# Moving the first six scalings of a float64-to-float32 weight conversion from ScalarE to GpSimd

## The chip, the cores and the metric

The kernel runs on one core of one Trainium2 chip. The metric is the device time of one execution in microseconds (us). Three runs of the kernel before gave 615.62, 618.41 and 619.05 us; the median is 618.41 us. The engines are named as the profile names them: PE (TensorE), PEld (its weight loads), DVE (VectorE), ACT (ScalarE), POOL (GpSimd) and SP (SyncE, which issues most DMAs). A trailing q (SPq) is an engine's queue.

## The reference, cut to what matters

Three layers follow each other: attention with capped scores (4 batches, 12 heads, 448 tokens, 64 per head), a feed-forward layer with a squared ReLU (768 to 2048 to 768), and a soft mixture of 8 experts.

```python
scores = scale * np.matmul(q, k.transpose(0, 1, 3, 2))
scores = cap * np.tanh(scores / cap)
attn = softmax(scores)                 # written out in the reference
x = attn @ v                           # to (1792, 768)
h = x @ w_in                           # w_in, w_out: float64
r = np.maximum(h, 0.0)
x = (s * (r * r) + b) @ w_out
...                                    # soft mixture: phi, w1, w2
```

`w_in` and `w_out` arrive as float64. The kernel turns them into float32 itself, with integer operations on the two 32-bit words of each number.

## The kernel before, in words

**Attention.** Heads are taken in twelve groups of four, Q = 0 to 11, three for each batch. A group makes score tiles `sc` on PE (lines 148, 170, 178), their tanh on ACT (lines 158, 160, 182), the exponentials on ACT (line 220), their sum `es` on DVE (lines 229 and 233), the products with v in `U` on PE (line 261), the column sums `Sm` on PE, copied with a small constant added on ACT (line 246), a reciprocal on DVE (line 247) and a product that gives the group's part of x (lines 275 to 279). Queries and keys are first split into a high and a low half on DVE, later partly on ACT (lines 94 and 95). Queues run in order on every engine.

**Feed-forward.** For each batch, `hidden` runs 16 chunks of the 2048 columns. A chunk splits its slice of `w_in` (tile `wr`) into `ws`, high half on ACT (line 540), low half on DVE (line 541), and makes 18 products into `hp` on PE (line 557). The first of them needs the x of batch 0, that is groups Q = 0, 1, 2. The attention of the next batch is interleaved with the chunks of this one. Then come the last batch without attention, and a tail that reads the weights of the experts (tile `wt`, 48 transfers of 1 MB).

**Conversion.** `convert` (line 375 on) is a generator that is advanced between those steps. A unit is a tile `raw` of 128 x 768 float64 numbers, loaded by SP (line 391) into one of three buffers. ACT takes the high words as float32, scales them by 2 to the -112 and writes `wr` or `o` (line 397, `scale`). DVE masks and shifts the result (line 402, `first`), puts the sign back (line 426) and adds the low word's bits (line 430), which frees the raw buffer. There are 48 units: 16 slices of `w_in` (stored for the later batches at line 461), 16 halves of `w_out` transposed and 16 of `w_out`. The first six in the order of the program are `w_in` slices 0 and 1, the two halves of the first transposed `w_out` part (tile `o`), and `w_in` slices 2 and 3. Unit 4 in the program's count, the fifth, has a condition: it is issued after the instruction `self.mark`, the exponential of group Q = 2, chunk 3 (set in `expo`). The order of instructions on the engines is a scheduler's, from the dependencies and the priorities in the code.

Of the kernel before, what the change touches and what calls it, by code (L numbers as in the profile page):

```python
# [7 lines left out]
F32 = mybir.dt.float32  # L8
# [3 lines left out]
AF = mybir.ActivationFunctionType  # L12
ALU = mybir.AluOpType
# [34 lines left out]
CU = 768  # L48
LAY = (22, 3, 2)
HOLD = 4  # L50
FAR = 2
ORDER = (0, 2, 4, 1, 3, 5)
XPOS = (1, 4, 7, 10, 13, 15, 15, 15)
# [10 lines left out]
class Body:  # L64
# [184 lines left out]
    def weighted(self, Q, chunks):  # L249
# [6 lines left out]
        for k in order:  # L256
            for h in range(2):
                for i in range(4):
                    d = (i % 2 * KF + k if k < KF else 2 * KF) * D + 32 * h
                    j = 32 * (i ^ 2 * h if Q >= FAR * NQ else i)  # L260
                    products.append(lambda k=k, h=h, i=i, j=j, d=d: nc.tensor.matmul(  # L261
# [4 lines left out]
    def finish(self, Q):  # L266
# [6 lines left out]
        with self.tc.high_priority(100) if Q < NQ else nullcontext():  # L273
            if Q < FAR * NQ:
                nc.vector.tensor_mul(out, u, self.rec[:, None, :].to_broadcast([P, 2, S]))
# [103 lines left out]
    def convert(self, units):  # L379

        nc = self.nc
        N = len(units)
        raw, out = {}, {}

        def load(n):
            if n < N:
                raw[n] = self.cv.tile([P, CU, 2], I32, tag="raw", bufs=self.raws, name="raw")  # L390
                nc.sync.dma_start(raw[n].rearrange("p a b -> p (a b)"), units[n][0].bitcast(I32))

        def scale(n):
            if n < N:
                out[n] = units[n][1]()
                with self.tc.issue_after(self.mark) if n == 4 and self.mark else nullcontext():
                    nc.scalar.activation(out[n], raw[n][:, :, 1].bitcast(F32), AF.Copy, scale=2.0 ** -112)  # L397

        def first(n):
            if n < N:  # L400
                o = out[n].bitcast(I32)
                nc.vector.tensor_scalar(o, o, 0x0FFFFFFF, 3, op0=ALU.bitwise_and, op1=ALU.logical_shift_left)

        for n in range(self.raws - 1):
            load(n)
        for n in range(N + 1):
            if n:
                units[n - 1][2](out.pop(n - 1))
            late = n < N and n not in out
            for _ in range(HOLD if self.later and late else 0):  # L410
                yield
            while self.later and (late or n == N):
                self.later.pop(0)()
                yield
            if late:
                while not units[n][3]():
                    yield
                scale(n)
                first(n)
            load(n + self.raws - 1)  # L420
            ahead = n + 1 < N and units[n + 1][3]()
            if ahead:
                scale(n + 1)
            if n < N:
                o = out[n].bitcast(I32)
                nc.vector.scalar_tensor_tensor(o, raw[n][:, :, 1], -0x80000000, o, op0=ALU.bitwise_and, op1=ALU.bitwise_or)  # L426
            if ahead:
                first(n + 1)
            if n < N:
                nc.vector.scalar_tensor_tensor(o, raw.pop(n)[:, :, 0], 29, o, op0=ALU.logical_shift_right, op1=ALU.bitwise_or)  # L430
            yield
            while self.later:
                self.later.pop(0)()
                yield
# [77 lines left out]
    def w_need(self, i):  # L512
# [6 lines left out]
        else:  # L519
            self.wr[i] = self.raw_slice()  # L520
            src, n = self.wsc[i % FC] if self.f64 else self.io["w_in"][i % FC], KC * P // 2
            if i < FAR * FC:
                self.nc.sync.dma_start(self.wr[i], src)
# [581 lines left out]
```

## Time and profile before

| what | value |
|---|---|
| median of three runs | 618.41 us (615.62 to 619.05) |
| the profiled execution's own time | 618.13 us |
| its span, first to last instruction | 616.3 us |
| PE, DVE, ACT, POOL busy | 573.2, 382.7, 394.2, 4.1 us |
| mean granted TensorE clock | 0.984 |
| chain that ended last, by engine | PE 47%, DMA 17%, DVE 16%, ACT 13%, issue 5% |

The span is 1.8 us shorter than the execution's own time; what lies around it is the same start and end for both kernels. The shares of busy time are averages over stages that have different limits, so the table is only a beginning: which engine has no free time is read stage by stage. "Idle before" in a row is the time in which the engine stood still ahead of that instruction, with what ended it behind the arrow.

### The profile page before, as it was taken

Reading aid. Unit: us, or ns where it says so; the run is one execution under the profiler, and the core shown is the slowest. Engines: PE = TensorE matmul, PEld = TensorE weight load, DVE = VectorE, ACT = ScalarE, POOL = GpSimd, SP = SyncE. Lnnn points to the kernel's source line nnn. Section 1 sums busy time; section 2 is a strip of 40 time slices with the busy share of each in tenths; the row PEclk is TensorE's granted clock in tenths of the full one; section 3 lists DMA queues with packets and bytes.
Section 4 is the critical chain, followed back from the end, with each engine's and each line's share of the span. In section 5 each row is a group of like instructions: output and inputs, shape, how many; then the busy total and the mean of one; then the engine's idle time right before and its main releaser. Section 6 shows DMA issues by size and latency. Waiting matters only on the chain.

```text
span 616.3 us, 11164 instructions
## 1 busy us (share of the span) xinstructions
PE 573.2 (93%) x4488; PEld 386.5 (63%) x4488; DVE 382.7 (62%) x569; ACT 394.2 (64%) x611; POOL 4.1 (1%) x11
## 2 busy tenths in 40 slices
PE   7898999999999999989999999999999998999663
PEld 5243575657677576566875675858788874348543
DVE  4999999999894978748829867462422224213212
ACT  5899889889769688488697696946455541012001
POOL 1000000000000000000000000000000000000000
PEclk9999999999999999989999999999999999999977
DMA  8844768686684665556655632214979989999997
GB/s 293 282 136 144 265 237 294 223 296 220 203 293 155 223 214 160 171 199 194 202 186 173 208 118 75 69 53 151 349 256 307 342 316 365 417 420 414 420 412 279
DMA packets 49995, 149.97 MB, mean 243 GB/s; under 512 B 5504, under 2 KB 27792, under 8 KB 43024
## 3 DMA queue, kind: packets, MB, share of 16 engines
q1 hardware_dynamic: 49648, 148.66, 68.5%
q8 instruction: 37, 0.61, 0.4%
q0 software_dynamic: 288, 0.53, 0.2%
q14 instruction: 22, 0.18, 0.1%
HBM read 131.07 MB, written 18.09 MB: 242 GB/s over the span
## 4 chain that ended last, share of the span: by engine, by line
PE 47%; DMA 17%; DVE 16%; ACT 13%; issue 5%; SPq 1%; DVEq 0%; ACTq 0%
PE hp L557 24%; DMA wt<-in_w_dram 12%; PE U L261 6%; ACT e L220 4%; PE pt L682 2%; PE tp L587 2%; ACT e L182 2%; DVE ws L541 2%; ACT e L158 2%; PE sc L148 2%; DVE o L426 2%; PE sc L178 2%; DVE es L229 2%; PE L L601 1%; DVE rec L247 1%
## 5 line engine op out<-in xcount | busy, mean ns | idle before, releaser
L557 PE MATMUL hp<-x,ws 128*128 128x448 f32 x1152 | 269.2, 377 | 0.0
L557 PEld LDWEIGHTS hp<-x,ws 128*128 128x128 f32 x1152 | 208.1, 189 | 45.7 <-issue 30.6
L541 DVE TENSOR_TENSOR ws<-wr,ws 128x384 fp32r<-128x384 f32 x128 | 70.4, 553 | 88.1 <-ACT ws L540 81.1
L540 ACT CAST ws<-wr 128x384 fp32r<-128x384 f32 x128 | 65.6, 518 | 39.0 <-PE hp L557 38.3
L261 PE MATMUL U<-e,v 128*32 128x448 f32 (+1 forms) x672 | 69.0, 542 | 4.7 <-ACT e L220 3.6
L220 ACT ACTIVATE e<-e,c_acap 128x1792 f32<-128x1792 f32 (+1 forms) x42 | 71.2, 1696 | 0.5
L261 PEld LDWEIGHTS U<-e,v 128*32 128x32 f32 (+1 forms) x672 | 20.5, 109 | 42.9 <-issue 32.7
L590 ACT COPY g<-tp 128x384 f32<-128x384 f32 (+1 forms) x64 | 34.4, 538 | 13.2 <-PE tp L587 7.4
L565 ACT ACTIVATE r<-hp 128x448 f32<-128x448 f32 x63 | 34.4, 545 | 11.0 <-PE hp L557 9.9
L158 ACT ACTIVATE e<-sc,c_tsc 128x896 f32<-128x896 f32 x36 | 35.5, 1005 | 8.9 <-PE sc L148 8.9
L182 ACT ACTIVATE e<-sc,c_tsc 128x896 f32<-128x896 f32 x36 | 35.8, 1024 | 5.7 <-PE sc L178 5.5
L247 DVE RECIPROCAL rec<-rec 128x448 f32<-128x448 f32 x12 | 35.4, 2948 | 5.0 <-ACT rec L246 4.9
L566 ACT ACTIVATE r<-r 128x448 f32<-128x448 f32 x63 | 37.1, 588 | 0.5
L397 ACT ACTIVATE o<-raw 128x768 f32<-128x768 f32 x32 | 29.1, 931 | 12.2 <-DVE c_hh L693 7.4
L958 PE MATMUL so_ps<-wt,free 128*32 128x128 f32 x768 | 27.7, 295 | 9.2 <-DMA wt<-in_w_dram 9.2
L587 PE MATMUL tp<-c_cst,r 128*128 128x128 f32 x192 | 32.6, 277 | 3.6 <-ACT g L590 2.8
L942 ACT COPY wt<-op 128x512 f32<-128x512 f32 (+1 forms) x12 | 6.8, 568 | 42.6 <-PE op L937 42.5
L229 DVE TENSOR_TENSOR es<-e 128x1792 f32<-128x1792 f32 x12 | 24.3, 2022 | 14.1 <-ACT e L220 14.1
L587 PEld LDWEIGHTS tp<-c_cst,r 128*128 128x128 f32 x192 | 23.9, 141 | 12.7 <-ACT g L590 4.7
L430 DVE SCALAR_TENSOR_TENSOR o<-raw,o 128x768 int32<-128x768 int32 x32 | 30.4, 952 | 0.4
L426 DVE SCALAR_TENSOR_TENSOR o<-raw,o 128x768 int32<-128x768 int32 x32 | 30.4, 953 | 0.3
L958 PEld LDWEIGHTS so_ps<-wt,free 128*32 128x32 f32 x768 | 21.8, 117 | 13.3 <-DMA wt<-in_w_dram 9.5
(187 smaller groups left out, 695.0 us busy)
## 6 DMA issues: line engine op xcount, KB each, us to landing
wt<-in_w_dram SPq DMA_DIRECT2D x48, 1024.0 KB, 14.6
raw<-in_w_in_dram SPq DMA_DIRECT2D x16, 768.0 KB, 5.7
raw<-in_w_outT_dram SPq DMA_DIRECT2D x16, 768.0 KB, 5.8
raw<-in_w_out_dram SPq DMA_DIRECT2D x16, 768.0 KB, 5.7
wsc<-wr SPq DMA_DIRECT2D x16, 384.0 KB, 2.8
wr<-wsc SPq DMA_DIRECT2D x16, 384.0 KB, 3.4
osc<-o SPq DMA_DIRECT2D x16, 384.0 KB, 3.5
wr<-wsc SPq DMA_DIRECT2D x32, 192.0 KB, 3.2
```

Source lines behind the costliest of these rows:

```text
L158: nc.scalar.activation(self.e[Q][c][:, 2 * j:2 * j + 2, :], sc[:, :, :S], AF.Tanh, scale=self.c["tsc"])
L182: nc.scalar.activation(self.e[Q][c][:, 2 * j:2 * j + 2, :], sc[j][:, :, :S], AF.Tanh, scale=self.c["tsc"])
L220: ins = self.nc.scalar.activation(e, e, AF.Exp, scale=self.c["acap"]).ins
L247: nc.vector.reciprocal(self.rec, self.rec)
L261: products.append(lambda k=k, h=h, i=i, j=j, d=d: nc.tensor.matmul(self.U[j:j + 32, h, :S], self.v[2 * Q + i // 2][self.rows(i, k), d:d + ...
L426: nc.vector.scalar_tensor_tensor(o, raw[n][:, :, 1], -0x80000000, o, op0=ALU.bitwise_and, op1=ALU.bitwise_or)
L540: self.nc.scalar.copy(hi, u)
L541: self.nc.vector.tensor_sub(lo, u, hi.bitcast(F32))
L557: nc.tensor.matmul(hp[:, :S], ws[kc // 3][:, w, kc % 3, :], x[ORDER[kc] // 2][:, s, ORDER[kc] % 2, :], start=(k == 0), stop=(k == 3 * KC - 1))
L566: self.mark = nc.scalar.activation(r2, r2, AF.Square).ins
L587: nc.tensor.transpose(tp[:, q * P:(q + 1) * P], r2[:, 64 * odd + q * P:64 * odd + (q + 1) * P], self.c["idn"])
L958: nc.tensor.matmul(so_ps[32 * e:32 * e + 32, G, :], ht[G][:, f, 32 * e:32 * e + 32], w2[f // 4][:, f % 4, e, :], start=(f == 0), stop=(f = ...
```

## The change

In the conversion's `scale`, the first six units (n = 0 to 5) are scaled by a GpSimd `tensor_scalar` multiplication by the same constant; the other 42 stay on ACT. The condition on the fifth unit is gone. Nothing else is edited.

```diff
+SIDE = 6
...
         def scale(n):
             if n < N:
                 out[n] = units[n][1]()
-                with self.tc.issue_after(self.mark) if n == 4 and self.mark else nullcontext():
-                    nc.scalar.activation(out[n], raw[n][:, :, 1].bitcast(F32), AF.Copy, scale=2.0 ** -112)
+                if n < SIDE:
+                    nc.gpsimd.tensor_scalar(out[n], raw[n][:, :, 1].bitcast(F32), 2.0 ** -112, None, op0=ALU.mult)
+                    return
+                nc.scalar.activation(out[n], raw[n][:, :, 1].bitcast(F32), AF.Copy, scale=2.0 ** -112)
```

The scheduler moves other instructions too. In the listings below the changed file's lines are numbered 1 to 3 higher than before's (line 220 is 221, line 402 is 405, line 430 is 433), and the numbers behind names tell buffers apart.

POOL, from its last start-up DMA on, before:

```order
L1024 DMA c_misc_100<-in_phi_dram 128x192
L1035 TENSOR_LOAD c_flag_90
L1036 COMPARE_AND_BRANCH
L853 DMA c_misc_100<-in_cst_dram 128x256
L875 DMA free_5080<-in_cst_dram 128x256
```

and now:

```order
L1027 DMA c_misc_100<-in_phi_dram 128x192
L1038 TENSOR_LOAD c_flag_90
L1039 COMPARE_AND_BRANCH
L398 ISA
L398 TENSOR_SCALAR wr_243<-raw_239 128x768
L398 TENSOR_SCALAR wr_248<-raw_241 128x768
L398 TENSOR_SCALAR o_309<-raw_246 128x768
L398 TENSOR_SCALAR o_309<-raw_307 128x768
L398 TENSOR_SCALAR wr_708<-raw_361 128x768
L398 TENSOR_SCALAR wr_715<-raw_706 128x768
```

[...]

ACT in the first group of heads, from the exponential of chunk 0 to that of chunk 2, before:

```order
L220 ACTIVATE e_209<-e_209,c_acap_87 128x1792
L158 ACTIVATE e_235<-sc_228,c_tsc_92 128x896
L158 ACTIVATE e_235<-sc_253,c_tsc_92 128x896
L397 ACTIVATE wr_243<-raw_239 128x768
L220 ACTIVATE e_235<-e_235,c_acap_87 128x1792
L397 ACTIVATE wr_248<-raw_241 128x768
L158 ACTIVATE e_286<-sc_279,c_tsc_92 128x896
L158 ACTIVATE e_286<-sc_289,c_tsc_92 128x896
L397 ACTIVATE o_309<-raw_246 128x768
L220 ACTIVATE e_286<-e_286,c_acap_87 128x1792
```

and now:

```order
L221 ACTIVATE e_209<-e_209,c_acap_87 128x1792
L159 ACTIVATE e_235<-sc_228,c_tsc_92 128x896
L159 ACTIVATE e_235<-sc_253,c_tsc_92 128x896
L221 ACTIVATE e_235<-e_235,c_acap_87 128x1792
L159 ACTIVATE e_286<-sc_279,c_tsc_92 128x896
L159 ACTIVATE e_286<-sc_289,c_tsc_92 128x896
L221 ACTIVATE e_286<-e_286,c_acap_87 128x1792
```

Three scalings are gone from between the attention's own instructions here, a fourth a few rows later, and the two that stood behind the marked exponential as well.

DVE in the same place, from the first unit's mask to the second sum, before:

```order
L402 TENSOR_SCALAR wr_243<-wr_243 128x768
L426 SCALAR_TENSOR_TENSOR wr_243<-raw_239,wr_243 128x768
L430 SCALAR_TENSOR_TENSOR wr_243<-raw_239,wr_243 128x768
L229 TENSOR_TENSOR es_201<-e_209,e_235 128x1792
L402 TENSOR_SCALAR wr_248<-wr_248 128x768
L94 CAST qh_327<-q2_215 128x448
L426 SCALAR_TENSOR_TENSOR wr_248<-raw_241,wr_248 128x768
L402 TENSOR_SCALAR o_309<-o_309 128x768
L430 SCALAR_TENSOR_TENSOR wr_248<-raw_241,wr_248 128x768
L229 TENSOR_TENSOR es_201<-es_201,e_286 128x1792
```

and now:

```order
L405 TENSOR_SCALAR wr_243<-wr_243 128x768
L429 SCALAR_TENSOR_TENSOR wr_243<-raw_239,wr_243 128x768
L230 TENSOR_TENSOR es_201<-e_209,e_235 128x1792
L405 TENSOR_SCALAR wr_248<-wr_248 128x768
L433 SCALAR_TENSOR_TENSOR wr_243<-raw_239,wr_243 128x768
L429 SCALAR_TENSOR_TENSOR wr_248<-raw_241,wr_248 128x768
L405 TENSOR_SCALAR o_309<-o_309 128x768
L433 SCALAR_TENSOR_TENSOR wr_248<-raw_241,wr_248 128x768
L230 TENSOR_TENSOR es_201<-es_201,e_286 128x1792
```

DVE has the same instructions in both kernels; here the first unit's last step has moved behind the first sum, and one cast of queries behind the second.

## Rows read from the trace of the kernel before

**Rows 1.** The page: the span in 40 slices, busy share in tenths.

```profile
PE   7898999999999999989999999999999998999663
DVE  4999999999894978748829867462422224213212
ACT  5899889889769688488697696946455541012001
POOL 1000000000000000000000000000000000000000
DMA  8844768686684665556655632214979989999997
```

**Rows 2.** Busy time by stage: us, then busy (count) of PE, PEld, DVE, ACT, POOL; clock, DMA share, GB/s.

```profile
16.00:64.00 48.00, 42.72 (x341) 17.71 (x340) 46.84 (x55) 43.93 (x47) 0.00 (x0) 1.00 0.58 187
64.00:140.00 76.00, 75.37 (x483) 48.11 (x483) 74.49 (x94) 66.05 (x98) 0.00 (x0) 1.00 0.76 261
140.00:260.00 120.00, 116.88 (x808) 78.56 (x808) 95.78 (x134) 92.28 (x148) 0.54 (x1) 1.00 0.61 209
416.00:525.00 109.00, 106.24 (x672) 81.84 (x670) 32.76 (x81) 53.03 (x110) 0.54 (x1) 1.00 0.85 299
525.00:616.00 91.00, 68.08 (x1101) 44.98 (x1100) 18.70 (x50) 10.99 (x18) 0.00 (x0) 0.91 0.98 394
```

**Rows 3.** Waits of DVE between 15 and 140 us: us in total, times, longest.

```profile
DVE wr L402 <- ACT wr L397: 3.5, 3, 3.1
DVE rec L247 <- ACT rec L246: 0.6, 1, 0.6
DVE c_hh L488 <- PE pf L487: 0.2, 1, 0.2
```

**Rows 4.** Timeline of DVE at the first units and reciprocals: start us, us, instruction.

```profile
11.62 0.69 DVE L95 TENSOR_TENSOR kl<-k,kh 128x512 fp32r<-128x512 f32 x1
15.43 0.56 DVE L402 TENSOR_SCALAR wr<-wr 128x768 int32<-128x768 int32 x1 [3.12 <-ACT wr L397]
16.03 0.96 DVE L426 SCALAR_TENSOR_TENSOR wr<-raw,wr 128x768 int32<-128x768 int32 x1
17.90 2.02 DVE L229 TENSOR_TENSOR es<-e 128x1792 f32<-128x1792 f32 x1
...
27.09 0.55 DVE L402 TENSOR_SCALAR o<-o 128x768 int32<-128x768 int32 x1
...
30.30 2.95 DVE L247 RECIPROCAL rec<-rec 128x448 f32<-128x448 f32 x1 [0.62 <-ACT rec L246]
...
63.09 2.95 DVE L247 RECIPROCAL rec<-rec 128x448 f32<-128x448 f32 x1
```

**Rows 5.** Timeline of ACT around its first scaling and the two held ones.

```profile
12.74 1.88 ACT L158 ACTIVATE e<-sc,c_tsc 128x896 f32<-128x896 f32 x2
14.52 0.89 ACT L397 ACTIVATE wr<-raw 128x768 f32<-128x768 f32 x1
...
58.02 1.69 ACT L397 ACTIVATE wr<-raw 128x768 f32<-128x768 f32 x2
...
66.67 1.01 ACT L158 ACTIVATE e<-sc,c_tsc 128x896 f32<-128x896 f32 x1 [2.25 <-PE sc L148]
```

**Rows 6.** Loads of raw tiles 0 and 3: issue on SP, and time to landing.

```profile
8.15 0.90 SPq L391 DMA_DIRECT2D raw<-in_w_in_dram  x2
...
raw<-in_w_in_dram SPq DMA_DIRECT2D x1, 768.0 KB, 6.2
...
18.44 1.00 SPq L391 DMA_DIRECT2D raw<-in_w_outT_dram  x1
...
raw<-in_w_outT_dram SPq DMA_DIRECT2D x1, 768.0 KB, 5.0
```

**Rows 7.** All scalings of `wr` on ACT, by form.

```profile
L397 ACT ACTIVATE wr<-raw 128x768 f32<-128x768 f32 x16 | 14.6, 922 | 3.1 <-DVE ws L541 1.5 <-DVE es L233 1.5
```

**Rows 8.** Timeline of POOL: its last start-up work and its next.

```profile
3.48 0.54 POOL L1024 DMA_DIRECT2D c_misc<-in_phi_dram  x1
214.82 0.54 POOL L853 DMA_DIRECT2D c_misc<-in_cst_dram  x1 [210.80 <-PE pp L479]
```

**Rows 9.** ACT and DVE in one stretch of 20 us (columns as in rows 2).

```profile
80.00:100.00 20.00, 19.75 (x128) 12.78 (x127) 19.49 (x24) 19.37 (x31) 0.00 (x0) 1.00 0.80 276
```

## The prediction

> **What bounds the kernel now.** I read the busy shares along the span first [rows 1], then the busy time by stage [rows 2], then DVE's waits and timeline in the stage that the change touches [rows 3, 4], and last the scalings themselves and the transfers that feed them [rows 5 to 7]. From slice 2 to slice 8 DVE stands at 9 tenths or more, while POOL stands at 0 from slice 2 on [rows 1]. The stages say it more sharply: from 16 to 64 us DVE works 46.84 of 48 us, from 64 to 140 us 74.49 of 76 [rows 2]. It works through its queue in order, so a stage in which it is idle for 1.16 or 1.51 us can't get shorter by more than that, unless DVE itself has less to do. Two other engines are close behind: ACT with 43.93 of 48 us, and PE, which from 64 us on is busy for 75.37 of 76 and then 116.88 of 120 us. Later stages belong to PE (416 to 525 us, 106.24 of 109) and to the transfers of the experts' weights (525 to 616 us, DMA share 0.98). Both start when what is ahead of them ends, so a shift before 140 us is passed on: DVE has 24 us of idle time from 140 to 260 us in which it could catch up, but PE there has 3.
>
> **What the change removes.** Six scalings leave ACT, at 0.922 us each [rows 7]: 5.5 us of its busy time. Four stood at the start of the first group of heads (the first at 14.52 us), the two held ones at 58.02 us [rows 5]. I cost this relief at nothing. What hides it is DVE: all exponentials that ACT would now finish earlier meet an engine without a free slot. Behind the two held ones ACT waits 2.25 us for PE at 66.67 us anyway [rows 5], more than the 1.69 us they took. If that cover were gone, the gain could be as much as the whole 5.5 us (a rival below).
>
> **What it adds on the path.** DVE's first mask waited 3.12 us for the first scaling, until 15.43 us [rows 3, 4]. The raw tile was issued at 8.15 us and took 6.2 us to land [rows 6]: POOL can't start before 14.35 us, ACT started at 14.52. The trace of before has no computing instruction on POOL beside start-up work [rows 8], so its price is bounded by DVE's rows: below by the mask, 0.56 us for the same 768 numbers, above by the sum of 1792 numbers, 2.02 us [rows 4]. I take 0.96 us, the row of line 426, because it is nearest in kind: it reads the same strided raw tile at the same length, one instruction per unit. The first mask then starts at 14.35 + 0.96 = 15.31 us, a gain of **0.1 us**; the ends give a gain of 0.5 and a loss of 0.9.
>
> [...]
>
> DVE's other idle time in that stage is 0.62 us ahead of the first reciprocal, for ACT's copy of the column sums [rows 3, 4]. With three exponentials earlier on ACT I let it go: **0.6 us** gained, none in the worst case.
>
> **Moved instructions.** DVE has the same work ahead of the third reciprocal in both orders, but for two splittings of the same length that changed places. In between, the second reciprocal now has the last two steps of unit 3 behind it instead of ahead, 1.9 us by the row of line 426. What is late instead are raw buffers. The load of unit 3 waits for unit 0's last step, which now stands behind a sum and a mask: 15.31 + 0.56 + 0.96 + 2.02 + 0.56 + 0.96 = 20.4 us instead of 18.4; with its 5.0 us to landing [rows 6] and 0.96 us on POOL it is ready at 26.4 us. DVE wanted it at 27.09 us [rows 4], and the same fourteen instructions stand ahead of that mask now. So this is hidden, by 0.6 us; the loads behind it in SP's queue are 2 us later too and wanted later still. The held units are not a gain: without the condition POOL may scale unit 4 as soon as it has landed, but DVE's three steps for units 4 and 5 stand around the third reciprocal in both orders. Together 0, with 1 us to either side.
>
> **The two engines at once.** Five scalings (units 1 to 5) fall into a stretch in which DVE works without a break. Here the bounds lie far apart: nothing if POOL and DVE run side by side, 5 x 2.02 = 10.1 us if DVE stands still for each at the upper price. I take 5 x 0.96 = **4.8 us** lost. DVE has no idle time into which a hold-up could fall, and it does not matter which engine is held: if POOL waits behind DVE, then DVE, in order, waits for POOL's result at the next mask, as it waited 3.12 us for ACT's.
>
> [...] POOL's rows show no such overlap either way [rows 8], and DVE's rows show 98% of busy time in the stretch [rows 2]. [...]
>
> **Sum**, against the profiled execution's own 618.13 us (span 616.3 us plus what lies around it; 0.3 us under the median of 618.41): 618.13 - 0.1 - 0.6 + 4.8 = **622.2 us**.
>
> **Rivals.**
> *Side by side.* POOL and DVE don't hinder each other. Then only the two small gains are left: 617.4 us, no change that can be seen. For it: the engines have queues of their own, and nothing in the trace shows POOL's few small instructions delaying anything. Against it: both read the same raw and `wr` tiles in a stretch in which DVE never pauses.
>
> *ACT is what ends the wait.* ACT's 5.5 us come back in full: 618.13 - 5.5 = 612.6 us, faster. It needs that DVE's busy row hides waiting for ACT, and it decides as soon as DVE's instructions of the first groups could run more than 3 us earlier than now. For it: ACT has 19.37 of 20 us from 80 to 100 us [rows 9], and every exponential and every high half passes through it. Against it: DVE has 19.49 us in the same stretch, and its waits for ACT from 15 to 140 us sum to some 4 us, 3.1 of them on the first unit, which the raw tile's landing keeps where it is.
>
> [...]
>
> That the change does not do what it says can be left aside: the order shows the six on POOL.
>
> **Chances.** What a measurement of this kernel can tell from no change is about 0.5%, 3.1 us, so the borders are 615.3 and 621.5 us. My forecast 0.48: 0.30 slower, 0.18 within the border, because the price of a scaling is a guess between ends and a part of it may fall under a reciprocal, which DVE runs for 2.95 us at a time. Side by side 0.27: 0.21 the same, 0.04 faster and 0.02 slower by what the new order does up to 260 us. ACT ends the wait 0.17: 0.16 faster, 0.01 the same. POOL not ready 0.08, all slower. Together faster 0.20, same 0.40, slower 0.40. The range is 613.5 to 627.5 us: its top is the sum with the upper price held back a little for reciprocals, and most of the late-code case, its bottom most of ACT's case; some 0.1 lies below it and some 0.07 above. The forecast's own range is 617.4 to 627.5 us.
>
> **What would show it.** In the profile after: POOL's six rows of line 398, the first at about 14.4 us and near 1 us long; DVE's first mask at 15.3 us. If the forecast holds, DVE rows that overlap those six are longer than their usual 0.56, 0.96 and 2.02 us or have gaps of that size ahead of them, and the third reciprocal, at 63.09 us before [rows 4], starts some 4 us later. If it starts within 1 us of 63.09, the engines run side by side. If it starts 3 us or more earlier, ACT was the bound and I was wrong about DVE. [...] The forecast is wrong as a whole if the time moves without DVE's third reciprocal moving: then it is made or lost behind 64 us, in the order of the scheduler.

## The result, and the profile after

The change makes the kernel slower: 622.08 us (median of 8 runs) against 617.27 us for the kernel before on the same chip, a ratio of 1.0082 with a 95% interval of 1.0061 to 1.0103, some 5 us. The forecast was 622.2 us and lay within the range. The profiled execution took 623.76 us (span 622.0 us); before it was 618.13 us and 616.3 us. In the listings of after, line 398 is POOL's scaling, 400 ACT's, 405 the mask, 429 and 433 the two steps behind it, 230 the first sum `es`, 248 the reciprocal.

The busy shares of after, 40 slices, answer to [rows 1]:

```profile
PE   8699999999989999999999999999999998999775
DVE  4889989999984986758839968372422223213212
ACT  5588699888858879479689496946555641002001
POOL 1522000000000000000000000000000000000000
PEclk9889999999999999999999999999999998999875
```

POOL is now busy in the second to fourth slices, and there DVE and ACT have dropped. The table by stage (columns as in [rows 2]) says by how much:

```profile
16.00:64.00 48.00, 40.41 (x288) 15.84 (x288) 43.39 (x49) 35.31 (x38) 15.54 (x6) 0.93 0.48 164
64.00:140.00 76.00, 74.57 (x495) 45.49 (x497) 72.22 (x91) 65.25 (x93) 0.00 (x0) 1.00 0.72 246
140.00:260.00 120.00, 115.97 (x808) 78.25 (x802) 97.41 (x137) 93.29 (x148) 0.60 (x1) 1.00 0.63 217
```

From 16 to 64 us DVE works 43.39 us where it worked 46.84 [rows 2]: an engine that had 1.2 us of idle time has 4.6. ACT went from 43.93 to 35.31 us, and nothing came of it. The waits of DVE between 15 and 140 us name what it now waits for (columns as in [rows 3]):

```profile
DVE wr L405 <- POOL wr L398: 5.5, 1, 5.5
DVE o L405 <- POOL o L398: 2.1, 1, 2.1
DVE es L230 <- ACT e L221: 1.9, 2, 1.1
DVE rec L248 <- ACT rec L247: 1.7, 4, 0.6
```

POOL's timeline of after, its six scalings (start, us, instruction, idle before; [rows 8] answer to them):

```profile
15.50 4.35 POOL L398 TENSOR_SCALAR wr<-raw 128x768 f32<-128x768 f32 x2 [11.46 <-DMA raw<-in_w_in_dram]
19.82 2.20 POOL L398 TENSOR_SCALAR o<-raw 128x768 f32<-128x768 f32 x1
29.15 3.62 POOL L398 TENSOR_SCALAR o<-raw 128x768 f32<-128x768 f32 x1 [7.12 <-DMA raw<-in_w_outT_dram]
32.74 2.16 POOL L398 TENSOR_SCALAR wr<-raw 128x768 f32<-128x768 f32 x1
49.72 3.76 POOL L398 TENSOR_SCALAR wr<-raw 128x768 f32<-128x768 f32 x1 [14.82 <-DVE ws L544]
```

DVE's timeline of after, in the same stretch and at the third reciprocal (answers to [rows 4]):

```profile
17.73 1.23 DVE L405 TENSOR_SCALAR wr<-wr 128x768 int32<-128x768 int32 x1 [5.50 <-POOL wr L398]
19.00 0.96 DVE L429 SCALAR_TENSOR_TENSOR wr<-raw,wr 128x768 int32<-128x768 int32 x1
19.87 2.74 DVE L230 TENSOR_TENSOR es<-e 128x1792 f32<-128x1792 f32 x1
...
23.00 0.95 DVE L433 SCALAR_TENSOR_TENSOR wr<-raw,wr 128x768 int32<-128x768 int32 x1
...
29.79 0.95 DVE L429 SCALAR_TENSOR_TENSOR o<-raw,o 128x768 int32<-128x768 int32 x1
32.80 1.22 DVE L405 TENSOR_SCALAR o<-o 128x768 int32<-128x768 int32 x1 [2.07 <-POOL o L398]
...
35.32 2.95 DVE L248 RECIPROCAL rec<-rec 128x448 f32<-128x448 f32 x1 [0.44 <-ACT rec L247]
...
68.96 2.95 DVE L248 RECIPROCAL rec<-rec 128x448 f32<-128x448 f32 x1 [0.39 <-ACT rec L247]
```

Three things are to be read from these two timelines.

First, the price: a scaling takes 2.16 to 2.20 us on POOL where nothing holds it (ACT: 0.92 us [rows 7]).

Second, DVE's rows that start beside a POOL row are longer: the mask at 17.73 us 1.23 us for 0.56, the sum at 19.87 us 2.74 for 2.02, the mask at 32.80 us 1.22 for 0.55. That is 0.67, 0.72 and 0.67 us, 2.06 us in all. The step at 19.00 us, which starts in the middle of one, is not: it keeps its 0.96 us while POOL is at work from 17.7 to 19.8 us.

Third, the other way round POOL waits, as I read it: its row of 29.15 us lasts 3.62 us. DVE's rows follow each other without a gap until 30.7 us, and from there to POOL's end at 32.77 us it is 2.1 us, the price alone.

The path up to the first reciprocal then closes, from 30.30 [rows 4] to 35.32 us, 5.02 us later. The first mask is 2.30 us late: POOL started at 15.50 us, ACT at 14.52 (0.98 us, because a part of raw tile 0 landed late in this execution, see the last experiment on the change), and the mask came 2.23 us behind that start instead of 0.91. The three long rows add 2.06 us, the wait for unit 3 2.07 us. Three splittings that stood ahead of this reciprocal now stand behind it (1.25 us, from 28.43 to 29.68 us of the profile before), and the wait for the column sums is 0.44 us for 0.62: 2.30 + 2.06 + 2.07 - 1.25 - 0.18 = 5.0 us. What ended last here were the column sums, on a PE with a granted clock of 0.50 from 28 to 32 us (the first two `Sm` products took 1.70 us at 28.15 us, and 0.94 us at a clock of 1.00 before), and DVE's own rows 0.44 us ahead of them. In the two other profiles of this order (below) DVE goes into this reciprocal without a wait, at 33.88 and 33.95 us, 3.6 us late, and there the sum closes with DVE's rows alone: 1.2 + 2.15 + 2.15 - 1.25 - 0.62 = 3.6 us. At the third reciprocal, 63.09 us before [rows 4], it is 5.87 us. The last product into `hp` starts at 507.39 us for 502.72, so 4.7 of them are still there; the stages between, in which PE has few free microseconds (1.4 of 76 and 4.0 of 120), pass them on.

### The profile page after: what moved, and what is told of

It is laid out like the page before. It is cut to its first block, busy times and chain, and to the rows that moved or that the text cites. A ratio compares the mean times of both kernels' runs of the same rounds, so it can differ in the third digit from the quotient of the medians.

```text
span 622.0 us, 11171 instructions
## 1 busy us (share of the span) xinstructions
PE 581.2 (93%) x4488; PEld 391.1 (63%) x4488; DVE 384.5 (62%) x569; ACT 390.5 (63%) x605; POOL 20.2 (3%) x17
## 4 chain that ended last, share of the span: by engine, by line
PE 46%; DVE 16%; DMA 16%; ACT 14%; issue 5%; SPq 1%; POOL 0%; ACTq 0%; DVEq 0%
PE hp L560 22%; DMA wt<-in_w_dram 12%; PE U L262 6%; ACT e L221 3%; PE pt L685 3%; DVE rec L248 2%; ACT e L183 2%; PE tp L590 2%; PE sc L149 2%; DVE ws L544 2%; DVE es L230 2%; PE Sm L242 2%; PE sc L179 2%; DVE o L429 2%; ACT o L400 2%
## 5 line engine op out<-in xcount | busy, mean ns | idle before, releaser
L400 ACT ACTIVATE o<-raw 128x768 f32<-128x768 f32 x30 | 27.2, 930 | 14.7 <-DVE c_hh L696 7.3
```

## The experiments

Theory A: the loss is POOL itself, that is, its 2.2 us waited for in order, and the 0.7 us by which it lengthens DVE's rows. Rival B: the loss is the condition's removal, which lets the scheduler set an order that costs more. Each comparison is with the kernel before on the same chip (617.3 to 617.7 us).

**Unit 0 back on ACT.**

```diff
-                if n < SIDE:
+                if 0 < n < SIDE:
```

> The change with unit 0 back on ACT; units 1 to 5 stay on POOL, no condition. Theory 1 (DVE, in order, waits for POOL's 2.2-us scalings, and the first raw tile lands 1 us late): ACT's 0.92 us in place of POOL's 2.20 takes 1.3 us off DVE's first mask (17.73 us to about 16.4), the wait of about 2 us at unit 3 stays: about 620.8 us, between before and after. Theory 2 (the loss is DVE and POOL holding each other up while both work): unit 0's scaling found DVE idle and held nobody up, so nothing changes: about 622 us.

Measured: 622.49 us, ratio 1.0065 (1.0041 to 1.009): theory 1's 620.8 us is missed, theory 2's 622 us came out. The first mask came back to 15.74 us, and unit 3's mask started at 30.01 us without a wait, but the third reciprocal stood at 69.38 us. DVE's waits of that kernel show where the gain went:

```profile
DVE rec L248 <- ACT rec L247: 4.9, 4, 3.6
DVE wr L405 <- ACT wr L400: 3.5, 1, 3.5
...
DVE wr L405 <- POOL wr L398: 0.5, 1, 0.5
```

DVE's waits for POOL fell from 7.6 us to 0.5, and the time did not follow. The first reciprocal waited 3.6 us for the column sums instead. Two things, as I read it, made these late: the second sum `es`, which they need, ended at 27.44 us (24.83 before) behind three long DVE rows, and the granted clock was 0.88, 0.50 and 0.77 in the three stretches of 4 us from 24 to 36 us (1.00 before). So the waits on POOL aren't the whole loss: with the other five on POOL, taking them away is worth no more than the measurement can tell, and this run doesn't show what they cost by themselves.

**The condition alone.** The changed kernel with `SIDE = 0`: all units on ACT, none held back.

```diff
-SIDE = 6
+SIDE = 0
```

> Only the condition is taken away; all scalings stay on ACT, nothing on POOL. Theory 1 (DVE bounds the first 140 us, ACT has time to spare): within 1 us of before, 616.3 to 618.3 us. Rival (ACT is what ends the waits, and the condition kept its queue free): the two scalings stand among the first groups' exponentials and cost their 1.7 us or more, 619 us or above.

Measured: 621.5 us, ratio 1.0059 (1.0039 to 1.0079). No POOL row, and still some 3.6 us lost. The prediction costed the removal at nothing. ACT's timeline shows what it does there:

```profile
33.20 1.01 ACT L159 ACTIVATE e<-sc,c_tsc 128x896 f32<-128x896 f32 x1
34.10 0.90 ACT L400 ACTIVATE wr<-raw 128x768 f32<-128x768 f32 x1
34.90 1.90 ACT L159 ACTIVATE e<-sc,c_tsc 128x896 f32<-128x896 f32 x2
...
41.61 0.95 ACT L400 ACTIVATE wr<-raw 128x768 f32<-128x768 f32 x1
```

Units 4 and 5 are scaled at 34.10 and 41.61 us instead of at 58.02 us [rows 5], among the tanh and exponentials of the second group, and DVE's steps for them follow early. DVE's waits for ACT's `rec` up to 70 us grew from 0.6 to 3.0 us. But 1.95 us of them stand at the first reciprocal, ahead of the first instruction that has moved on ACT (34.10 us), DVE or PE:

```profile
31.59 2.95 DVE L248 RECIPROCAL rec<-rec 128x448 f32<-128x448 f32 x1 [1.95 <-ACT rec L247]
```

Up to there the order is that of before, and the granted clock was 0.81 from 20 to 24 us and 0.76 from 24 to 28, where it was 1.00 before. That part belongs to the clock of this execution and not to the order. The ratio, from 7 runs, made B a serious rival all the same.

**Units 4 and 5 alone on POOL.**

```diff
-                if n < SIDE:
+                if 4 <= n < SIDE:
```

> Units 0 to 3 on ACT as before, units 4 and 5 on POOL, no condition. Theory 1: these two have 10 us and more before DVE wants them, so no wait for POOL; if loading POOL's code is what made the first raw tile land 1 us late, DVE's first mask comes at about 16.4 us and the time is 617.5 to 619 us; if not, 616.5 to 617.5 us. Rival (ACT's relief is worth its 1.7 us): 615.6 us. Theory 2 (each scaling on POOL costs DVE about 1 us): 619 us or above with the first mask at 15.4 us.

Measured: 619.94 us, ratio 1.0041 (1.0022 to 1.006), above theory 1's 616.5 to 617.5 us and within theory 2's "619 us or above". The third reciprocal stands at 64.42 us, 1.3 us late. One DVE row beside POOL is long, a cast of 0.39 us that took 1.05 (0.67 us of the loss; where the rest comes from this run doesn't show):

```profile
41.18 1.05 DVE L95 CAST qh<-q 128x448 fp32r<-128x448 f32 x1
```

**POOL beside an unchanged order.** The kernel before, and for the first six units one more scaling on POOL into a scratch that nobody reads. DVE, ACT and PE keep the order of before throughout, and DVE waits for nothing of POOL's.

```diff
                 with self.tc.issue_after(self.mark) if n == 4 and self.mark else nullcontext():
                     nc.scalar.activation(out[n], ...)
+                if n < 6:
+                    nc.gpsimd.tensor_scalar(self.c["tmp"][:, :CU], raw[n][:, :, 1].bitcast(F32), 2.0 ** -112, None, op0=ALU.mult)
```

> The kernel before, with ACT's scalings and the condition as they were; in addition POOL makes the first six scalings into a tile that nobody reads. Nobody waits for POOL's result (a raw buffer is only given back when POOL has read it too). Theory 1 (waiting for results and the late first tile are the loss): about 1 us for the tile and up to 0.7 us for each DVE row that POOL delays, 618.5 to 620 us. Theory 2 (the engines hold each other up): as slow as the change, 622 us. If POOL and DVE did not touch at all: 617.3 us.

Measured: 620.23 us, ratio 1.0046 (1.0024 to 1.0067). This is the hold-up by itself, some 2.8 us; about 0.5 us of it lies outside the span from first to last instruction (2.3 us between span and time, 1.7 to 1.9 in the other kernels). DVE's timeline, of the slowest of the 12 executions (624.54 us):

```profile
17.21 1.66 DVE L432 SCALAR_TENSOR_TENSOR wr<-raw,wr 128x768 int32<-128x768 int32 x1
18.79 2.01 DVE L229 TENSOR_TENSOR es<-e 128x1792 f32<-128x1792 f32 x1
20.72 1.23 DVE L404 TENSOR_SCALAR wr<-wr 128x768 int32<-128x768 int32 x1
...
24.38 2.71 DVE L229 TENSOR_TENSOR es<-es,e 128x1792 f32<-128x1792 f32 x1
...
29.82 1.62 DVE L432 SCALAR_TENSOR_TENSOR o<-raw,o 128x768 int32<-128x768 int32 x1
31.36 0.82 DVE L94 CAST qh<-q 128x448 fp32r<-128x448 f32 x1
...
37.83 1.15 DVE L94 CAST x<-c_hh 128x896 fp32r<-128x896 f32 x1
```

Four rows that start just as a POOL row gets going are longer, by 0.70, 0.68, 0.69 and 0.66 us, and two casts that start some 0.6 us before a POOL row ends, by 0.43 and 0.52: 3.7 us in all. The wait of 0.62 us at the first reciprocal is gone, and the third moved from 63.09 to 66.10 us. Beside six POOL rows, 15.1 us together, DVE's rows took 3.7 us longer. Neither "side by side" nor a DVE that stands still for each POOL row is what happened.

**The condition kept, on POOL.** The changed kernel with the condition around unit 4's scaling on POOL.

```diff
                 if n < SIDE:
-                    nc.gpsimd.tensor_scalar(out[n], ...)
+                    with self.tc.issue_after(self.mark) if n == 4 and self.mark else nullcontext():
+                        nc.gpsimd.tensor_scalar(out[n], ...)
                     return
```

> The changed kernel with its six units on POOL, but unit 4 again issued only after the marked exponential. Theory A (POOL's 2.2 us per scaling, waited for in order, and the DVE rows that it lengthens by 0.7 us carry the loss): 622 us, within 1 us, third reciprocal near 69 us. Rival B (the removed condition carries most of it, since removing it alone cost 3.6 us): 619 us or less, third reciprocal under 66 us. Seen in the rows: with the condition no scaling of units 4 and 5 should start before some 58 us.

Measured: 622.84 us, ratio 1.0083 (1.0055 to 1.0111), third reciprocal at 67.51 us. The time is as A said, but units 4 and 5 were not held back:

```profile
14.39 4.45 POOL L399 TENSOR_SCALAR wr<-raw 128x768 f32<-128x768 f32 x2 [10.36 <-DMA raw<-in_w_in_dram]
18.82 2.19 POOL L399 TENSOR_SCALAR o<-raw 128x768 f32<-128x768 f32 x1
28.32 3.50 POOL L399 TENSOR_SCALAR o<-raw 128x768 f32<-128x768 f32 x1 [7.32 <-DMA raw<-in_w_outT_dram]
31.80 2.17 POOL L399 TENSOR_SCALAR wr<-raw 128x768 f32<-128x768 f32 x1
48.27 3.73 POOL L399 TENSOR_SCALAR wr<-raw 128x768 f32<-128x768 f32 x1 [14.29 <-DVE ws L545]
```

I expected nothing of them before 58 us; they run at 31.80 and 48.27 us. The instructions of PE, DVE, ACT and POOL come in the order of the change, one by one. The marked instruction is in ACT's queue, unit 4 no longer is: that the condition orders only what stands in that queue is my reading of it. So this run can't tell A from B by itself, but it settles something else. In the change, the condition's removal does nothing: once unit 4 is on POOL it holds nothing back.

**The first four units alone on POOL**, the held two on ACT with their condition.

```diff
+                if n < 4:
+                    nc.gpsimd.tensor_scalar(out[n], raw[n][:, :, 1].bitcast(F32), 2.0 ** -112, None, op0=ALU.mult)
+                    return
                 with self.tc.issue_after(self.mark) if n == 4 and self.mark else nullcontext():
```

> Units 0 to 3 on POOL, units 4 and 5 on ACT with the condition, as before the change. Theory A: the first mask 1.3 us later than before (POOL's 2.2 us for ACT's 0.9 us), unit 3 waited for by some 2 us, two DVE rows lengthened by 0.7 us: 1.3 + 2.1 + 1.4 = 4.8 us, and less if the extra landing time of raw tile 0 is a part of it; 621 to 622.5 us. Rival B: 618.5 us or less.

Measured: 621.08 us, ratio 1.0055 (1.0034 to 1.0077). B, 618.5 us or less, falls: with the condition at work the larger part of the loss is there. The first mask at 17.12 us, DVE's waits for POOL of 4.9 and 2.1 us, and two long rows (1.27 and 2.72 us) are those of the change. With units 4 and 5 alone at 1.0041, the two parts add up to 0.96%, against 0.82% (0.61 to 1.03) for both.

**The late units on POOL**, where DVE has time: the kernel before, its last 24 units on POOL.

```diff
+                if n >= 24:
+                    nc.gpsimd.tensor_scalar(out[n], raw[n][:, :, 1].bitcast(F32), 2.0 ** -112, None, op0=ALU.mult)
+                    return
                 with self.tc.issue_after(self.mark) if n == 4 and self.mark else nullcontext():
```

> The kernel before with its last 24 units on POOL instead of the first six; the condition stays. There DVE is busy for 47.6 of 60 us (140 to 200 us) and less later, and PE for 58.4 of 60. Theory A: each row of POOL alone is again 2.2 us and DVE rows beside it are again some 0.7 us longer, 24 x 0.7 = 17 us of DVE's idle time at most, but nothing of it reaches PE: 617 to 618.5 us. Rival (the hold-ups reach the path wherever they lie): 617.7 + 17 = 634 us. Rival (ACT's relief of 24 x 0.92 = 22 us is worth something there): at best the 1.5 us per 60 us in which PE stands still, some 4 us, 613.5 us.

Measured: 640.63 us, ratio 1.0349 (1.0319 to 1.0378). All three expectations missed; mine, "nothing of it reaches PE", by 22 us. DVE's waits from 140 to 420 us, then PE's:

```profile
DVE o L405 <- POOL o L397: 30.4, 12, 6.2
```

```profile
PE hp L560 <- DVE ws L544: 8.9, 6, 3.3
```

Before, DVE waited 9.3 us for these `o` tiles in the same stretch, seven times. The two halves of an `o` tile come in pairs, and a pair takes 4.35 us on POOL and 1.8 on ACT. DVE, in order, stands still at the mask (5.26 us ahead of the one at 234.70 us, with the next low half `ws` behind it at 237.33), and PE waits for these low halves of the running chunk; the list of before has no wait of this kind. DVE's free time there did not cover it, because it is not at the place where the wait falls. These 8.9 us are less than half of the 23 us lost; the rest was not traced.

**The change once more**, for the late part of raw tile 0.

> The changed kernel once more. If the late landing of raw tile 0 (15.4 us) belongs to the change (its code load in POOL beside the first loads), it is there again; if it was that one execution, the tile lands at 14.3 to 14.8 us, the first mask starts at 16.6 to 17.1 us instead of 17.7, and the time is 621 to 623 us all the same, within what executions differ by.

Measured: 623.99 us in one run, 1 us above the expected range. The tile landed at 14.35 us, POOL started at 14.44 and the first mask at 16.69 us. So the late landing (15.41 us) belonged to that one execution (no load of POOL's code shows in the profiles of before and after: the two instruction queues moved 0.61 and 0.18 MB in both), and the mask's true delay is 1.2 to 1.3 us, as in the kernel with the condition kept (16.61 us). The third reciprocal stands at 68.53 us.

**Units 1 and 2 on POOL**, the two with time to spare.

```diff
+                if n in (1, 2):
+                    nc.gpsimd.tensor_scalar(out[n], raw[n][:, :, 1].bitcast(F32), 2.0 ** -112, None, op0=ALU.mult)
+                    return
                 with self.tc.issue_after(self.mark) if n == 4 and self.mark else nullcontext():
```

> Only the two units on POOL whose masks had some 2 us of lead over their scaling on ACT (units 1 and 2); units 0, 3, 4, 5 stay on ACT with the condition. Theory A (waits in order for POOL's 2.2 us, and some 0.7 us per DVE row that starts beside a POOL row): next to no wait is left (the scaling ends by 19.5 us, its mask came at 19.83 us before), two rows are longer: 617.7 + 1.4 = 619.1 us, first mask at 15.4, third reciprocal near 65 us. Rival (DVE and POOL exclude each other for whole instructions, 2.2 us each): 622 us. Rival (side by side): 617.7 us.

Measured: 618.61 us, ratio 1.0031 (1.0009 to 1.0053), near the 619.1 us of A; the rival of 2.2 us lost for each row (622 us) lies outside the interval, and "side by side" (1.0000) only just. The two long rows are there:

```profile
17.05 1.62 DVE L433 SCALAR_TENSOR_TENSOR wr<-raw,wr 128x768 int32<-128x768 int32 x1
19.19 1.23 DVE L405 TENSOR_SCALAR wr<-wr 128x768 int32<-128x768 int32 x1 [0.53 <-POOL wr L397]
```

The path between is not what I expected: the third reciprocal came at 66.74 us, not near 65. The first one waited 3.02 us for the column sums; the granted clock was 0.60 from 28 to 32 us, where it was 1.00 before. That is 3.65 us late, but the execution (619.31 us) was only 1.2 us longer than the profiled one of before: behind 64 us a part came back.

**Six extra scalings on ACT**, the twin of the run beside the unchanged order.

```diff
                     nc.scalar.activation(out[n], ...)
+                if n < 6:
+                    nc.scalar.activation(self.c["tmp"][:, :CU], raw[n][:, :, 1].bitcast(F32), AF.Copy, scale=2.0 ** -112)
```

> The kernel before with six extra scalings on ACT, into a scratch that nobody reads, behind the real ones of the same units: 5.5 us more work on ACT in the stage of the change (the scheduler moves neighbours a little). If ACT's time there is worth nothing (the prediction's term of 0 for the relief): 617.7 to 618.5 us. Rival (ACT is as close to the path as DVE, so that where a scaling stands in its queue counts): 617.7 + 5.5 = 623 us at the most, with DVE waiting for ACT's rec and e rows.

Measured: 620.33 us, ratio 1.0045 (1.0024 to 1.0067): 2.8 us for 5.5 us of work, between the two theories. DVE's wait for `rec` is 3.8 us for 0.6. ACT is not free there. How much of this is the work itself, how much the order, which the scheduler changed with it, and how much the granted clock (0.85, 0.50 and 0.80 in the stretches of 4 us from 20 to 32 us) this run doesn't tell.

**A price list of POOL rows.** The kernel before, and nine POOL rows behind unit 24.

```diff
+                w = CU // 2 if n % 3 else CU
+                if 24 <= n < 33 and n % 3 == 1:
+                    nc.gpsimd.tensor_scalar(out[n][:, :w], raw[n][:, :w, 1].bitcast(F32), 2.0 ** -112, None, op0=ALU.mult)
...
+                if 24 <= n < 33 and n % 3 != 1:
+                    nc.gpsimd.tensor_scalar(out[n][:, :w], out[n][:, :w], 1.0, None, op0=ALU.mult)
```

> A price list, in the kernel before: nine extra POOL rows behind unit 24, where DVE has idle time; three multiply the finished 768 numbers of a tile by 1 in place (no gaps between them), three the first 384 of them, three scale the first 384 of the raw tile's high words (every second word). Rows of POOL with no DVE row beside their start: if the 2.2 us of the change come from reading every second word, 768 without gaps take 1.2 us or less and 384 with gaps 1.1 us; if it is POOL's speed for any 32-bit row, 768 without gaps take 2.2 us and both halves 1.1 us, plus a fixed part if there is one.

One run, 620.46 us. POOL's timeline (line 398 reads every second word, line 402 reads without gaps); these are the rows that DVE's rows did not hold back:

```profile
173.42 2.13 POOL L402 TENSOR_SCALAR o<-o 128x768 f32<-128x768 f32 x1 [11.06 <-ACT o L400]
...
183.45 1.16 POOL L402 TENSOR_SCALAR o<-o 128x384 f32<-128x384 f32 x1
195.82 1.19 POOL L398 TENSOR_SCALAR o<-raw 128x384 f32<-128x384 f32 x1 [11.21 <-PE pp L484]
...
221.64 1.17 POOL L402 TENSOR_SCALAR o<-o 128x384 f32<-128x384 f32 x1 [0.48 <-issue]
```

768 numbers without gaps take 2.13 us (2.16 to 2.20 with gaps, in the change), 384 take 1.16, and with gaps 1.19. This last figure is one row: the two others of its kind, issued while DVE's rows followed each other, took 2.32 and 2.30 us. So the gaps cost next to nothing here (0.03 us at 384 and up to 0.07 at 768): it is POOL's speed. Between 384 and 768 numbers (1.17 us and 2.18 us) it is 1.01 us for 384, 2.6 ns for each, with an estimated 0.16 us fixed (1.17 less 1.01). DVE's mask takes 0.56 us for the same 768.

**What the runs leave open.** The run beside the unchanged order shows 0.46% (0.24 to 0.67) of the change's 0.82% with nothing but POOL's rows added. The rest, some 2 us, is argued from the timelines: DVE's waits for POOL and the new order share it, and no run separates them. Other orders cost time without POOL too (0.59% with the condition gone, 0.45% with six more scalings on ACT), and no run has the new order without POOL's rows. That the new order itself costs something stays an untested rival.

## Why the prediction was right, and where its steps were not

The time (622.2 forecast, 622.08 measured) and its sign were right, and so was the place: an almost full DVE in the stage of the first groups, held by POOL and waiting for it in order. The third reciprocal was to start some 4 us later and started 4.4, 5.4 and 5.9 us later in three profiles of this order. But three terms were off, and their errors cancel. That the time came within 0.1 us is luck: the shift was forecast at 4.1 us, from an execution of 618.13 us, and measured at 4.8, from a median of 617.27.

*The price of a scaling* failed: "I take 0.96 us", with 2.02 as the upper end. It is 2.2 us, above the upper end. Both bounds were rows of DVE, and they did not bound POOL's.

*The first mask* therefore did not gain 0.1 us: it lost 1.2 to 1.3 us, and 2.3 in the execution with the late tile.

*Unit 3*, "hidden by 0.6 us", was waited for by 2.07 us. The chain was the right one and each link longer: the first mask 2.4 us behind the forecast's 15.31 us and two rows lengthened by 0.67 and 0.72 us put unit 0's last step's end at 23.95 us instead of 20.4, its buffer was loaded by 29.15 us, and POOL then had to let DVE finish first. The prediction used POOL's price once here and not the hold-ups of its own last term.

*The two engines at once*, 5 x 0.96 = 4.8 us, was too much: three rows and 2.06 us in the change, 3.7 us in the run that shows the hold-up alone. Of the five scalings counted, units 1, 2 and 4 have a long DVE row beside them; unit 3's (29.15 us) let DVE's rows go first, which is a part of the 2.07 us, and unit 5's (49.72 us) waited for a run of DVE's rows to end at 51.35 us and then ran beside a reciprocal. No run shows the 4.8 us, or a DVE that stands still for each scaling: the rows that start just as a POOL row of 2.2 us gets going are longer by 0.67 to 0.72 us each, and the step at 19.00 us, which starts in the middle of one, keeps its 0.96 us. On POOL's side the hold-up is longer: the rows of 29.15 and 49.72 us ended only 2.1 us after DVE's runs of rows.

*ACT's relief at nothing* held: 8.6 us less work on ACT from 16 to 64 us, about 4.5 of it scalings and the rest work that now comes later, and no gain in the time. The reason given, that DVE hides it, is only half tested, since six scalings more on ACT do cost 2.8 us.

*The condition* costs nothing in this change, as forecast, but not because DVE's steps stay where they are. As I read it, it held only ACT's queue, and the unit left that queue. On ACT its removal costs 3.6 us.

Of the rivals, "side by side" falls with the long rows, "ACT is what ends the wait" with ACT's 35.31 us and no gain. POOL not ready (0.08 of the chances) did not come true, and no run shows the late code that the range allows for: in all three profiles of the change's order the first scaling starts within 0.1 us of the tile's landing. Of the signs named ahead, the first POOL row came at 14.4 us where the tile landed in time, and the lengthened rows and the late third reciprocal came too; "near 1 us long" and a first mask at 15.3 us did not.

## What to carry to other kernels

Work moved to an idle engine is costed by that engine's own rows; where the trace has none, the bound from another engine's rows may be none (here 2.2 us, above the 2.02), and a run that only measures the price is the first thing to make. The offload to POOL, ahead of a DVE that works in order, cost twice here: by POOL's longer row at the next wait (2.2 us for ACT's 0.92, read from the timelines) and by DVE's rows beside it (some 0.7 us each, shown by a run of its own); busy shares with room in them, as in the late units, don't show whether there is room at that wait. And a total that comes out right says little of its terms: here three were wrong by 1.4 to 2.7 us each.

## What the runs showed of the hardware

POOL's and DVE's rows took longer beside each other, in an uneven way. A DVE row that started just as a POOL row got going took 0.66 to 0.79 us longer, whether it was a mask of 0.56, a step of 0.96 or a sum of 2.02 us. In the price list four rows that start 0.2 to 0.5 us behind POOL's were longer by 0.31 to 0.63 us. Rows in the middle of one, such as the step at 19.00 us with its 0.96 us, were not; the two late casts in the run beside the unchanged order are the exception. A reciprocal and a POOL row ran side by side: with the late units on POOL, a reciprocal from 169.86 us took its 2.94 us and the POOL row issued within it, at 170.72, its 2.19.

POOL rows that were issued while DVE's rows followed each other without a gap took longer in part. In the change two of them lasted 3.6 and 3.8 us instead of 2.2 and ended 2.1 us after DVE's run of rows; with unit 0 back on ACT one lasted 4.2, but two others, at 2.66 and 2.81 us, got in between two DVE rows.

The granted clock was not the same in executions of one instruction order. From 24 to 32 us, first in the change, then in the kernel with the condition kept (columns as in [rows 2]):

```profile
24.00:28.00 4.00, 1.96 (x14) 0.37 (x10) 4.00 (x4) 3.26 (x5) 0.00 (x0) 0.96 0.81 260
28.00:32.00 4.00, 3.85 (x14) 1.20 (x14) 2.73 (x6) 0.69 (x1) 2.85 (x1) 0.50 1.01 404
```

```profile
24.00:28.00 4.00, 2.57 (x14) 0.53 (x14) 4.00 (x6) 2.23 (x4) 0.00 (x0) 1.00 0.99 334
28.00:32.00 4.00, 3.87 (x29) 1.27 (x30) 1.84 (x4) 1.78 (x3) 3.67 (x2) 1.00 0.91 355
```

In the first, PE stood still for 2.0 of the first 4 us, and the next 4 us had a granted clock of 0.50; in the second it stood still for 1.4 us and the clock stayed at 1.00. In the repeat of the change the clock fell earlier, to 0.59 from 24 to 28 us. Standing still alone doesn't settle it: the kernel before and the kernel without the condition have the same order up to there, PE was busy for 2.86 and 2.85 us of the 4 from 16 to 20 us, at the full clock in both, and from 20 to 24 us the first kept 1.00 and the second got 0.81. With the full clock the third reciprocal came at 67.51 us instead of 68.53 and 68.96, and that execution took 623.01 us instead of 623.99 and 623.76: from these three executions I estimate that the clock carries 1 us or so of the change's cost, not the bulk of it. How far it explains the waits for the column sums where fewer units were on POOL, no run here settles.
